# Attention weights transposed by DMA instead of TensorE, and a new order of the pieces with little elementwise work on GpSimd

## The chip, the core and the metric

The kernel runs on one core of a Trainium2 chip. TensorE (PE in the profile; PEld is its loading of weights) multiplies matrices into PSUM, VectorE (DVE), ScalarE (ACT) and GpSimd (POOL) work elementwise, SyncE (SP) and GpSimd issue most DMAs. Each engine takes its own instructions in order, and engines wait for each other through semaphores. The metric is the device time of one execution in microseconds (us); lower is better.

## What is computed

For each of 8 batches and 8 heads, x (512 x 64) reads the state (32 x 64) through a softmax, and the state reads x through another. Both results together are the 4352 tokens of a feed-forward layer with a squared relu. Cut to what matters:

```python
scores = scale * (x @ state.T)            # rows: softmax over the 32 states
xread  = softmax(scores) @ state
scores2 = scale * (state @ x.T)           # columns: softmax over the 512 positions
sread  = softmax(scores2) @ x
tokens = concat(xread, sread)             # per batch 512 + 32 rows of 512
out = (s * relu(tokens @ w_in)**2 + b) @ w_out
```

The second softmax, over the columns of the scores, is the one that the change touches.

## The kernel before, in words

The kernel is cut into pieces, each a small function in a table (`pieces`, near the end), and a list of words, `ORDER`, nine strings long, says in which order they are emitted. Each engine gets its instructions in that order; a letter at a word's end (A, V, G) says on which engine an elementwise piece runs. The framework sets the semaphores.

Per batch b, and with 128 partitions throughout:

- x is loaded twice on GpSimd's DMA queue: as `xh` (for the scores; piece x, L188) and as `xn` (positions on partitions; piece xn, L197, four DMAs of 128 KB). Two buffers each.
- Row softmax: `xT` (DVE transposes 32 x 32 blocks, L302), `T` (scores, PE), `U`, `mu`, `D`, `E1`, `z`, `At`, `A` on DVE and ACT (Dm and At sometimes on GpSimd, L336 and L357).
- Column softmax: `nm`, `nms`, `E2` (exponentials with row sums, ACT, L390), `a2` (the weights, normed, 128 x 1024 fp16, DVE, L397 and L399). Then the weights must have positions on partitions: `aps` turns 128 x 128 blocks on PE against an identity (eight matmuls into a PSUM bank, L141 by the helper), `a2T` copies the bank to SBUF (L156, on ACT seven times, on DVE once), and `V` multiplies with xn (PE tile vps). `srd` copies the result (ACT, L435).
- The state is multiplied with w_in once (`M`, PE tile mps, and `Mc`, its copy to SBUF, L156), so layer 1 is two matmuls of 512 columns for each 128 features: piece `l.b.f` (L472) with its relu on ACT (L476). `s.b.f.n.E` squares n such blocks (L482 on DVE and GpSimd, L480 on ACT).
- Layer 2: batches 0 and 1 plainly (`L`, L516, four pieces for each row block; `out` evicts and stores). Batches 2 to 7 by a scheme with seven products of half blocks instead of eight: `S.b.i.h.E` makes sums of blocks (L586), `P.b.u` is one product in halves (14 pieces of eight matmuls, PE tiles opf_X, opf_Y, opf_W), `ev` evicts a bank after a product (DVE, L615), `put` stores (SP). The bank X is used by four products one after the other, each continuing what is in it: a product waits for the eviction before it.
- At the end the 256 state rows go through the same two layers (`lsr`, `ssr`, `S_sr`, `P_sr`, `ev_sr`).

DMAs on SP (all stores of results but the last few) and on GpSimd (all loads but the first) each stand in the list's order on their queue.

Of the kernel before, what the change touches and what calls it, by code (L numbers as in the profile page):

```python
# [11 lines left out]
FP16 = mybir.dt.float16  # L12
# [70 lines left out]
def kernel(  # L83
# [321 lines left out]
    def at_aps(b):  # L405
        at[b]["aps"] = aps = blocks(two_banks(f"aps_{b}", FP16), 0)
        for g in range(NG):
            for c in range(SCH):
                transp(aps[:, SCH * g + c], at[b]["a2"][:, g, P * c : P * c + P])

    def at_a2T(b, e):
        copy(e, sm(b, "a2T", [P, NG * SCH, P], FP16, apool, 2), at[b]["aps"])
# [97 lines left out]
    ops_t = {}  # L510

    def layer2(tag, rr, q):
        if q == 0:
            ops_t[tag, rr] = ps_o.tile([P, DM], FP32, name=f"ops_{tag}_{rr}", tag="po")
        for f in range(4 * q, 4 * q + 4):
            nc.tensor.matmul(  # L516
                ops_t[tag, rr],
                G_t[tag][:, f, P * rr : P * rr + P],
                w_out_f(f),
                start=(f == 0),  # L520
                stop=(f == NKF - 1),
            )
# [74 lines left out]
    def product(b, u):  # L597
# [3 lines left out]
        first, last = bank not in [p[0] for p in PRODUCTS[:n]], bank not in [p[0] for p in PRODUCTS[n + 1 :]]  # L601
        lhs = block(b, *lhs) if lhs else fast(b, "S3")
        for k in range(4 * h, 4 * h + 4):
            w = fast_w[rhs][:, k] if isinstance(rhs, str) else w_block(*rhs)(k)
            for rr in range(2):
                mm(
                    fast(b, bank)[:, rr], lhs[:, k, P * rr : P * rr + P], w,
                    start=(first and k == 0 and rr == 0), stop=(last and k == NKF // 2 - 1 and rr == 1), skip=True,
                )
# [50 lines left out]
    def bias_sum(q):  # L660
        if q == 0:
            cps_t.append(two_banks("cps")[:, 0, :])
# [106 lines left out]
```

## Time and profile before

| | |
|---|---|
| time, median of 3 runs | 217.82 us (217.42 to 217.86) |
| span of the profiled execution, first to last instruction | 215.7 us |
| time outside the span | about 2.1 us, from the median of the runs; the profiled execution has no other time of its own |
| PE busy | 205.8 us |
| DVE busy | 179.6 us |
| ACT busy | 158.0 us |
| POOL busy (DMA issues among it) | 86.9 us |
| DMA packets | 22.43 MB in 23658 packets |

The profile gives for each engine the time in which one of its instructions ran. Rows of groups read: line of the kernel, engine, operation, output and input tile, shapes, count; then busy us and mean ns of one; then the idle time just before them and who ended it. Rows of the chain of work that ended last read: start, length, what. A row of the waits reads: who waited for whom, us in total, times, longest. Matmuls overlap in the records, so a mean of one matmul is longer than the time by which the next one follows; the chain shows the latter.

### The profile page before, as it was taken

To read this page: it belongs to the slowest core of one execution; us is meant where nothing else is said; L and a number is where in the kernel's file an instruction comes from. 1 tells how busy PE (TensorE), PEld (TensorE's weight loads), DVE (VectorE), ACT (ScalarE), POOL (GpSimd) and SP (SyncE) were. 2 spreads that over 40 slices of the span, in tenths; PEclk is the share of its full clock that TensorE was granted. 3 is DMA by queue.
4 is the path that set the end of the run, shared out by engine and by line. 5 is a ranking of instruction groups with operands and counts; after the bars stand their busy time and mean duration, and the time that the engine had idled before them with its cause. 6 is when DMAs were issued, how large, how long until landed. Compare 5 with 4: busy or idle time off the path is not lost.

```text
span 215.7 us, 4829 instructions
## 1 busy us (share of the span) xinstructions
PE 205.8 (95%) x1955; PEld 130.0 (60%) x1955; DVE 179.6 (83%) x277; ACT 158.0 (73%) x260; POOL 86.9 (40%) x94
## 2 busy tenths in 40 slices
PE   7489999999999999999999999999999999999992
PEld 2134343344444448767677677677766777888881
DVE  2997899999998799969998999999986874593661
ACT  4598886899899788799999887779768475734300
POOL 8554126445093033157437057007223308916400
PEclk9969999999999999999999999999999999999999
DMA  6999998127849719523900939608902600440045
GB/s 153 175 207 206 196 206 146 41 63 106 137 106 140 133 20 171 68 50 64 162 24 2 187 112 115 82 17 145 221 8 46 144 11 0 102 97 0 5 147 145
DMA packets 23658, 22.43 MB, mean 104 GB/s; under 512 B 4436, under 2 KB 17492, under 8 KB 23636
## 3 DMA queue, kind: packets, MB, share of 16 engines
q0 software_dynamic: 16848, 12.52, 41.3%
q1 hardware_dynamic: 5504, 8.66, 14.9%
q10 hardware_dynamic: 1284, 0.95, 1.7%
q8 instruction: 15, 0.25, 0.5%
q14 instruction: 7, 0.06, 0.1%
HBM read 25.72 MB, written 8.91 MB: 161 GB/s over the span
## 4 chain that ended last, share of the span: by engine, by line
PE 91%; DMA 3%; ACT 2%; POOL 1%; DVE 1%; issue 0%; POOLq 0%
PE hps L472 25%; PE opf_X L141 20%; PE ops L516 13%; PE opf_W L141 10%; PE opf_Y L141 5%; PE mps L141 5%; DMA w_in<-in_moe_w_in_dram 3%; PE hps_sr L472 3%; PE vps L141 2%; PE aps L141 2%; PE ops_sr_X L141 2%; PE T_None L141 2%; ACT M L156 1%; PE hph L141 1%; PE ops_sr_W L141 1%; PE dps L683 1%
## 5 line engine op out<-in xcount | busy, mean ns | idle before, releaser
L476 ACT ACTIVATE r<-hps 128x512 f16<-128x512 f32 x120 | 68.8, 603 | 25.6 <-PE hps L472 22.3
L472 PE MATMUL hps<-A,M 128*128 128x512 f16 x240 | 65.6, 380 | 0.1
L141 PEld LDWEIGHTS <-g 128*128 128x128 f16 x576 | 56.0, 98 | 15.2 <-issue 0.9
L472 PEld LDWEIGHTS <-M 128*128 128x128 f16 x240 | 21.4, 98 | 19.8 <-issue 6.0
L482 POOL TENSOR_TENSOR g<-r 128x1024 f16<-128x1024 f16 (+1 forms) x9 | 21.3, 2372 | 27.0 <-ACT r L476 22.8
L156 ACT CAST M<-mps 128x1024 f16<-128x1024 f32 x29 | 29.2, 1013 | 2.3 <-PE mps L141 1.9
L516 PE MATMUL ops<-w_out,g 128*128 128x512 f16 x128 | 30.7, 379 | 0.0
L197 POOL DMA_DIRECT2D xn<-in_x_dram x32 | 18.7, 604 | 14.8 <-PE vps L141 14.0
L141 PE MATMUL opf_X<-w_T,g 128*128 128x256 f16 x192 | 24.1, 273 | 0.0
L482 DVE TENSOR_TENSOR g<-r 128x1024 f16<-128x1024 f16 (+1 forms) x30 | 22.1, 754 | 1.6 <-ACT r L476 1.6
L586 DVE TENSOR_TENSOR g<-g 128x1024 f16<-128x1024 f16 (+1 forms) x31 | 22.1, 728 | 0.2
L516 PEld LDWEIGHTS <-g 128*128 128x128 f16 x128 | 12.4, 98 | 14.9 <-POOL g L482 0.2
L615 DVE SCALAR_TENSOR_TENSOR osx<-opf_X,sb_bc,bias_bc 128x512 f32<-128x512 f32 x18 | 13.3, 740 | 7.7 <-PE opf_X L141 7.4
L357 POOL TENSOR_TENSOR At<-E,rz 128x1024 f16<-128x1024 f16 x4 | 7.7, 1914 | 21.6 <-DVE rz L348 21.6
L480 ACT ACTIVATE g<-r 128x1024 f16<-128x1024 f16 (+1 forms) x11 | 15.8, 1444 | 0.2
L141 PE MATMUL mps<-w_in,stT 64*32 64x512 f16 x256 | 13.0, 397 | 1.6 <-DMA w_in<-in_moe_w_in_dram 1.3
L586 POOL TENSOR_TENSOR g<-g 128x1024 f16<-128x1024 f16 (+1 forms) x3 | 8.3, 2768 | 15.4 <-PE opf_X L141 8.1
L141 PE MATMUL opf_W<-w_out,g 128*128 128x256 f16 x96 | 12.4, 273 | 0.0
L141 PE MATMUL opf_W<-w_T,g 128*128 128x256 f16 x96 | 12.3, 273 | 0.0
L141 PE MATMUL opf_X<-w_out,g 128*128 128x256 f16 x96 | 12.1, 273 | 0.0
L141 PE MATMUL opf_X<-w_T,S 128*128 128x256 f16 x96 | 11.8, 273 | 0.0
L141 PE MATMUL opf_Y<-w_out,g 128*128 128x256 f16 x96 | 11.8, 273 | 0.0
(102 smaller groups left out, 310.4 us busy)
## 6 DMA issues: line engine op xcount, KB each, us to landing
out_dram<-osx SPq DMA_DIRECT2D x44, 128.0 KB, 2.4
xn<-in_x_dram POOLq DMA_DIRECT2D x32, 128.0 KB, 6.7
xh<-in_x_dram POOLq DMA_DIRECT2D x14, 256.0 KB, 5.2
w_in<-in_moe_w_in_dram POOLq DMA_DIRECT2D x8, 256.0 KB, 9.2
w_out<-in_moe_w_out_dram POOLq DMA_DIRECT2D x4, 512.0 KB, 13.3
out_dram<-osb SPq DMA_DIRECT2D x16, 64.0 KB, 1.9
out_dram<-osb SPq DMA_DIRECT2D x8, 128.0 KB, 2.4
xf<-in_x_dram SPq DMA_DIRECT2D x2, 256.0 KB, 3.7
```

The costliest lines, as they stand in the source:

```text
L141: return nc.tensor.matmul(out, lhsT, rhs, start=start, stop=stop, tile_position=tp, is_transpose=is_transpose, skip_group_check=skip,)
L156: (engine.copy if engine is nc.scalar else engine.tensor_copy)(out, in_)
L197: nc.gpsimd.dma_start(out=xn_t[b][32 * jh : 32 * jh + 32].rearrange("t h c d -> t h (c d)"), in_=x[b].rearrange("h (t jh c) d -> jh t h (c ...
L357: e.tensor_tensor(out, E1, over_n(rz), ALU.mult)
L472: nc.tensor.matmul(hps, lhsT, rhs, start=(i == 0), stop=(i == len(terms) - 1))
L476: nc.scalar.activation(R_t[tag, q][:, i], hps, AF.Relu)
L480: nc.scalar.activation(g, r, AF.Square)
L482: e.tensor_mul(g, r, r)
L516: nc.tensor.matmul(ops_t[tag, rr], G_t[tag][:, f, P * rr : P * rr + P], w_out_f(f), start=(f == 0), stop=(f == NKF - 1),)
L586: e.tensor_tensor(out, x, y, op)
L615: nc.vector.scalar_tensor_tensor(out, fast(b, name[0]), s_bc, out if plus else bias, ALU.mult, ALU.add)
L683: nc.tensor.matmul(dps, ones16[:, :P], ones16, start=True, stop=True)
```

## The change

Three things change.

1. `aps` and `a2T` are replaced by one piece, `tr`: one DMA on SP's queue that transposes the 128 x 1024 weights from SBUF to SBUF into the same tile a2T. It waits for a2 (DVE) and for the buffer of a2T (two of them; the V two batches of that order before). `V` waits for its landing.
2. `ORDER` is a new list. Its first words, up to the first pieces of layer 1 of batch 0, stay; all later pieces stand in another order, and most letters G are now V or A. GpSimd keeps one Dm and one At besides its DMAs. The transposes stand in the list away from the words of the xn loads.
3. So that the quarters of a layer-2 sum and the halves of a product can come in any order, the pieces count visits: the first visit of a bank starts the accumulation, the last one ends it.

Cut to its core:

```diff
-    def at_aps(b):
-        at[b]["aps"] = aps = blocks(two_banks(f"aps_{b}", FP16), 0)
-        for g in range(NG):
-            for c in range(SCH):
-                transp(aps[:, SCH * g + c], at[b]["a2"][:, g, P * c : P * c + P])
-
-    def at_a2T(b, e):
-        copy(e, sm(b, "a2T", [P, NG * SCH, P], FP16, apool, 2), at[b]["aps"])
+    def at_tr(b):
+        a2T = sm(b, "a2T", [P, NG * SCH, P], FP16, apool, 2)
+        nc.sync.dma_start_transpose(out=a2T, in_=at[b]["a2"].rearrange("p g s -> p (g s)"))
...
+    def visit(*key):
+        visits[key] = visits.get(key, 0) + 1
+        return visits[key]
...
     def layer2(tag, rr, q):
-        if q == 0:
+        v = visit("L", tag, rr)
+        if v == 1:
...
-                start=(f == 0),
-                stop=(f == NKF - 1),
+                start=(v == 1 and f == 4 * q),
+                stop=(v == NKF // 4 and f == 4 * q + 3),
```

The places of the list that the prediction walks through, in the changed order (the fifth string, around V.5.2, and the seventh, around V.6.0):

```
... l.4.7 nms.6.V s.4.6.2.A mu.6 P.3.6 E2.6.1 a2.2 P.3.7 E2.6.0 ev.3.X2 S.3.4.1.V tr.2 l.4.14 z.5 s.4.12.4.A
ev.3.W1 S.3.4.0.V xn.6 P.3.8 P.3.9 s.4.4.2.A l.4.8 l.4.11 M.5.1.1 ev.3.X3 At.5.V V.5.2 ...

... a2.0 tr.6 l.5.6 P.4.13 s.5.6.2.A l.6.2 s.5.12.2.A xn.0 Mc.6.1.A l.6.1 P.4.12 P.4.10 l.6.3
Mc.6.3.V P.4.11 tr.0 l.6.0 S.5.3.0.V P.5.0 S.5.1.0.V E1.7 ev.4.X4 s.5.14.2.V l.6.12 l.6.10 V.6.0 ...
```

The numbers of instructions that change engine, before and after: squares of 1024 columns on ACT 6 and 30, on DVE 27 and 10, on GpSimd 7 and 0; squares of 2048 on ACT 5 and 6, on DVE 3 and 4, on GpSimd 2 and 0; copies of M on ACT 29 and 25, on DVE 3 and 7; At on DVE 3 and 6, on GpSimd 4 and 1; sums of blocks on GpSimd 7 and 0; transposing matmuls 64 and 0.

More of the change, by code (lines that the diff above doesn't have):

```diff
@@ L508, in layer1_sr @@
         layer1("sr", f, [(w_in_f(k, f), srdT[:, k].rearrange("p n b -> p (n b)")) for k in range(NK)], B * Ns)
-    ops_t = {}
+    ops_t, visits = {}, {}
+    def visit(*key):
+        visits[key] = visits.get(key, 0) + 1
+        return visits[key]
     def layer2(tag, rr, q):
-        if q == 0:
+        v = visit("L", tag, rr)
+        if v == 1:
             ops_t[tag, rr] = ps_o.tile([P, DM], FP32, name=f"ops_{tag}_{rr}", tag="po")
@@ L600, in product @@
         bank, lhs, rhs = PRODUCTS[n]
-        first, last = bank not in [p[0] for p in PRODUCTS[:n]], bank not in [p[0] for p in PRODUCTS[n + 1 :]]
+        v, visits_all = visit("P", b, bank), 2 * sum(p[0] == bank for p in PRODUCTS)
         lhs = block(b, *lhs) if lhs else fast(b, "S3")
@@ L607, in product @@
                     fast(b, bank)[:, rr], lhs[:, k, P * rr : P * rr + P], w,
-                    start=(first and k == 0 and rr == 0), stop=(last and k == NKF // 2 - 1 and rr == 1), skip=True,
+                    start=(v == 1 and k == 4 * h and rr == 0),
+                    stop=(v == visits_all and k == 4 * h + 3 and rr == 1), skip=True,
                 )
@@ L660, in bias_sum @@
     def bias_sum(q):
-        if q == 0:
+        v = visit("cps")
+        if v == 1:
             cps_t.append(two_banks("cps")[:, 0, :])
@@ L667, in bias_sum @@
                 cps[32 * c : 32 * c + 32, :], ones16[:, 0:32], w_out_f(f),
-                start=(f < 4), stop=(f >= NKF - 4), tp=(0, 32 * c),
+                start=(v == 1), stop=(v == NKF // 4), tp=(0, 32 * c),
             )
@@ L728 @@
         "E1": at_E1, "z": at_z, "At": at_At, "A": at_A, "nm": at_nm, "nms": at_nms, "E2": at_E2, "a2": at_a2,
-        "aps": at_aps, "a2T": at_a2T, "V": at_V, "srd": at_srd, "M": at_M, "Mc": at_Mc,
+        "tr": at_tr, "V": at_V, "srd": at_srd, "M": at_M, "Mc": at_Mc,
         "lh": layer1_half, "sh": square_half, "l": layer1_x, "s": square, "lsr": layer1_sr,
```

117 rows, old and new, of the table ORDER are left out of this document.

## The prediction, made before the changed kernel was run

> **What bounds the kernel now.** I read four views, from the whole to the place. First the page: busy times, and the chain of work that ended last.
>
> ```profile
> span 215.7 us, 4829 instructions
> PE 205.8 (95%) x1955; PEld 130.0 (60%) x1955; DVE 179.6 (83%) x277; ACT 158.0 (73%) x260; POOL 86.9 (40%) x94
> PE 91%; DMA 3%; ACT 2%; POOL 1%; DVE 1%; issue 0%; POOLq 0%
> ```
>
> TensorE (PE) carries nine tenths of the chain. A busy PE is not yet a PE that never waits, so the second view is PE's waits after the head (from 25 us on), and the third the busy times by stage.
>
> ```profile
> PE mps L141 <- DVE M L156: 0.4, 1, 0.4
> ```
>
> ```profile
> core 0: us, PE busy (x) PEld busy (x) DVE busy (x) ACT busy (x) POOL busy (x), PEclk, DMA share, GB/s
> 25.00:160.00 135.00, 134.90 (x1284) 80.81 (x1284) 126.88 (x184) 115.55 (x184) 53.79 (x61) 1.00 0.62 104
> 160.00:211.60 51.60, 51.60 (x505) 41.44 (x503) 33.34 (x57) 24.90 (x49) 20.43 (x10) 1.00 0.25 62
> 211.60:216.00 4.40, 0.02 (x1) 0.00 (x0) 0.48 (x1) 0.00 (x0) 0.00 (x0) 1.00 0.44 121
> ```
>
> After the head PE waits for anybody once, for 0.4 us, and its clock is granted in full (1.00). From 25 to 211.6 us the time is the sum of PE's pieces, and nothing else. VectorE (DVE) is close behind: in 25 to 160 us it is idle for 135 - 126.88 = 8.1 us, ScalarE (ACT) for 19.5. So a change here is worth the PE work that it removes, less the waits that it brings back to PE. The last 4.4 us are one DVE instruction and a store; the change leaves that end as it is (the last product, its eviction, its store).
>
> **The change, part by part.** *The transposes leave PE.* Eight pieces named aps go, one for each batch, and nothing else leaves PE or comes to it: all other matmuls are the same ones in another order. In the chain in order of time each such piece stands with its own cost (the first, the dearest and the last of the eight):
>
> ```profile
> 55.57 0.45 PE aps L141 x8
> ...
> 104.49 0.55 PE aps L141 x8
> ...
> 178.14 0.45 PE aps L141 x8
> ```
>
> 8 x 0.45 = 3.6 us (3.7 with the dear one). All eight stand on the chain, one behind the other with PE's other work, so this comes off in full as long as PE stays fed. It is the only term that the change gains.
>
> *The copies out of PSUM, and GpSimd's elementwise work.* I counted instructions of each form on each engine in the changed kernel against the one before, and priced them with these rows:
>
> ```profile
> L156 ACT COPY a2T<-aps 128x1024 f16<-128x1024 f16 x7 | 7.1, 1015 | 0.0
> L156 ACT CAST M<-mps 128x1024 f16<-128x1024 f32 x29 | 29.2, 1013 | 2.3 <-PE mps L141 1.9 <-PE hps L472 0.3
> L480 ACT ACTIVATE g<-r 128x1024 f16<-128x1024 f16 x6 | 6.2, 1054 | 0.1
> L480 ACT ACTIVATE g<-r 128x2048 f16<-128x2048 f16 x5 | 9.6, 1912 | 0.1
> L480 ACT ACTIVATE g_sr<-r_sr 128x512 f16<-128x512 f16 x4 | 2.4, 625 | 0.6 <-PE opf_X L141 0.6
> L156 DVE CAST M<-mps 128x1024 f16<-128x1024 f32 x3 | 3.7, 1219 | 0.5 <-PE mps L141 0.5
> L357 DVE TENSOR_TENSOR At<-E,rz 128x1024 f16<-128x1024 f16 x3 | 3.9, 1303 | 0.1
> L482 DVE TENSOR_TENSOR g<-r 128x1024 f16<-128x1024 f16 x27 | 18.6, 703 | 1.6 <-ACT r L476 1.6
> L482 POOL TENSOR_TENSOR g<-r 128x1024 f16<-128x1024 f16 x7 | 13.9, 1990 | 17.0 <-ACT r L476 12.8 <-issue 4.2
> L482 POOL TENSOR_TENSOR g<-r 128x2048 f16<-128x2048 f16 x2 | 7.4, 3708 | 10.0 <-ACT r L476 10.0
> ```
>
> ACT: 24 more squares of 1024 (25.3 us), one more of 2048 (1.9), six more small ones (3.8), four casts of M fewer (-4.1), seven copies of a2T fewer (-7.1), one small copy fewer (-0.6): **+19 us**, to about 177. DVE: four more casts of M (4.9), three more At (3.9), seven more sums of blocks (about 4.9 at the 0.70 of a square of the same shape, the double one counted twice and the small ones half), one more square of 2048 (1.2), but 17 squares of 1024 fewer (-12.0) and three small ones (-1.3); with two small copies about **+1 us**, to about 181. GpSimd loses 22 squares, sums and At and keeps one At and one Dm. It was no bound: these two rows alone waited 22.8 us for ACT.
>
> This work lies beside PE, and its cover is PE's own stream. It costs nothing while each engine finishes its share before PE needs it. Total load leaves room (177 and 181 of 216), so what counts is the densest stretch. That is the list's fourth and fifth strings (first S.2.3.0 to last Mc.5.1). Records of one engine overlap at their ends; how fast instructions really follow each other is seen in the timeline of each engine, two relus and two sums of 1024 in a row:
>
> ```profile
> 66.79 1.08 ACT L476 ACTIVATE r<-hps 128x512 f16<-128x512 f32 x2
> ```
>
> ```profile
> 103.76 1.28 DVE L586 TENSOR_TENSOR g<-g 128x1024 f16<-128x1024 f16 x2
> ```
>
> Two relus of 0.60 take 1.08, so one follows another after 0.5: I take 0.1 off each ACT row; 0.08 off each DVE row in the same way. PE's pieces, from the chain again (two layer-1 pieces, one product, two M pieces):
>
> ```profile
> 54.71 0.86 PE hps L472 x4
> ...
> 88.68 0.87 PE opf_X L141 x8
> ...
> 93.91 0.56 PE mps L141 x16
> ```
>
> In that stretch PE has 25 products (21.9), 31 layer-1 pieces (13.3), three layer-2 pieces at two layer-1 pieces' cost (2.6) and about 6 us of M, T and V: 43 to 44 us. ACT has 31 relus (15.5), six casts (5.5), six squares of 1024 (5.7), six of 2048 (10.9) and some 6 us of exponentials and small copies: also 43 to 44. DVE's list there, added in the same way, gives the same. All three are full for 44 us. Before the change DVE ran at 126.88 / 135 = 94% without making PE wait; now ACT has that level too and the two pass work to each other. PE's waits there I bound from below at 0 (what the densest stage before showed, but for 0.4) and from above at about 5 (the 19 us that ACT gets, less the 19.5 that it had idle, would fit exactly; a quarter of it in the wrong place would not). I take **1 us**, near the row that shows a full engine costing almost nothing.
>
> *The transposing DMA.* Instead of eight matmuls and a copy, SP issues one DMA of 256 KB from SBUF to SBUF, and the piece V waits for its landing. The trace of before has no transposing DMA. The nearest rows, DMA issues with size and median time to landing:
>
> ```profile
> out_dram<-osx SPq DMA_DIRECT2D x44, 128.0 KB, 2.4
> xn<-in_x_dram POOLq DMA_DIRECT2D x32, 128.0 KB, 6.7
> xf<-in_x_dram SPq DMA_DIRECT2D x2, 256.0 KB, 3.7
> stn<-in_state_dram POOLq DMA_DIRECT2D x1, 192.0 KB, 12.7
> ```
>
> From 2.4 (it can gain nothing below zero: its landing is only ever waited for) to 12.7; I take 3.7, the row of the same queue and size. Does that fit? The tightest place is V.5.2, behind tr.2. After a2.2 DVE's queue has ev.3.X2 (0.74 by the row below), for which the product P.3.8 waits; then PE has P.3.8 and P.3.9 (1.75), two layer-1 pieces (0.86) and M.5.1.1 (0.3) before V.5.2.
>
> ```profile
> L615 DVE SCALAR_TENSOR_TENSOR osx<-opf_X,sb_bc,osx 128x512 f32<-128x512 f32 x6 | 4.5, 742 | 2.0 <-PE opf_X L141 1.8
> ```
>
> So V.5.2 comes at the earliest 0.74 + 1.75 + 0.86 + 0.3 = 3.7 us after a2.2, and a landing of 3.7 costs nothing. Behind tr.0, tr.7 and tr.1 PE has 6.9 to 7.4 us of pieces between the place of a2 and that of V; less a2's own 0.9 that is 6 us. Behind tr.3, tr.4, tr.5 and tr.6 there is more. Queued behind a transpose on SP stand only stores of results; the next batch's first eviction waits for those, some 5 us of PE's pieces later where it is closest, and a store lands in 2.4. On GpSimd the loads of xn now stand almost alone and can start earlier. All this I cost at 0.
>
> Sum against the profiled execution: span 215.7 - 3.6 + 1.0 = 213.1. The median of the runs shown, 217.82, lies 2.1 above that span, so 217.8 - 2.6 = **215.2 us**. With no wait at all and a few M and T pieces standing closer together it would be 213.8.
>
> **The rivals.** *The landing comes late (slower).* A landing of d us after a2 makes PE wait d - 3.7 at V.5.2 and d - 6 at each of V.6.0, V.7 and V.1. Nothing remains of the 2.6 us from d = 6.2 on (2.5 + 3 x 0.2 = 3.1; at 6.1 it is 2.7). At 6.7, the row of the xn loads that may run beside it, the waits are 3.0 + 2.1 = 5.1: 215.2 + 5.1 = 220.3. For it: no row shows a transpose, and both rows of GpSimd's queue lie above 6. Against it: both rows of SP's queue, on which the transposes are issued, lie under 4. I give it 0.25.
>
> *Far later.* At 12.7, the slowest row, the waits are 9.0 + 20.1 = 29: 244 us, and each further us adds four. [...] 0.05.
>
> *ACT and DVE become the bound.* PE's waits in the dense stretch reach the 3.6 us of the gain: 217.8, or somewhat above at the bound of 5 (219.2). For it: all three engines full for 44 us. Against it: DVE was as full before and cost PE 0.4. 0.12.
>
> *The transposes were hidden anyway* is excluded: all eight stand in the chain with their full 0.45.
>
> **How the numbers follow.** Forecast (213.8 to 217.0): 0.58. Late landing 0.25, far later 0.05, ACT and DVE the bound 0.12. A measurement of this kernel can tell about 0.2% (0.4 us). Faster: the forecast and a little of the third rival, 0.60. Same: half of that rival, 0.06. Slower: the rest, 0.34. The range runs from 213.8 to 222.0: below it nothing is reachable with the matmuls that remain, above it lie the far case and the part of the first rival with d over 7.1, together under 0.2. The forecast's own range is 213.8 to 217.0.
>
> **What would show it.** Right: the chain without aps and with no DMA named a2T in it; PE's waits after 25 us sum to about 1 us, on ACT's r and DVE's osx or g; a2T lands within 4 us of its issue; ACT near 177 less its overlaps, GpSimd under 45. Wrong: waits of the vps matmuls for a2T (the first rival, by its landing time), long waits of hps for r or of opf for g or S (the third), or transposes that slow the loads or stores beside them, for which I have no row.

## The result, and the profile after

The changed kernel took 214.99 us (median of 4 runs, 214.72 to 215.54) against 217.84 (217.42 to 218.11) of the kernel before in the same measurement: a ratio of 0.987, 95% interval 0.985 to 0.989, so faster by 1.3%. Its profiled execution has a span of 212.9 us. Here and in the table of the experiments a ratio leaves out runs more than 1.5% above the fastest of the same kernel; medians and ranges do not.

First the page of the changed kernel, in the order of the prediction: span and instructions, busy times, and the chain of work that ended last by engine.

```profile
span 212.9 us, 4690 instructions
PE 202.8 (95%) x1891; PEld 126.6 (59%) x1891; DVE 179.5 (84%) x272; ACT 170.9 (80%) x279; POOL 42.8 (20%) x72
PE 77%; DVE 9%; ACT 7%; DMA 3%; issue 1%; SPq 1%; DVEq 0%
```

PE has 64 instructions fewer (the transposing matmuls) and 3.0 us less busy time. ACT has 12.9 more, GpSimd 44.1 less. PE's share of the chain fell from 91% to 77%, which looks like a new bound and is none: the chain passes through ACT, DVE and one store wherever PE is released just in time. How long PE really waits stands in its waits from 25 us on:

```profile
PE mps L140 <- ACT M L155: 0.2, 1, 0.2
PE opf_X L140 <- DVE osx L615: 0.2, 1, 0.2
```

0.33 us in all (0.17 and 0.16), as little as the one wait before the change (0.37). The busy times by stage (columns as before: PE, PEld, DVE, ACT, POOL, granted clock, DMA share, GB/s):

```profile
25.00:160.00 135.00, 134.65 (x1250) 78.99 (x1248) 127.79 (x179) 124.93 (x199) 30.14 (x49) 1.00 0.68 115
160.00:209.00 49.00, 48.45 (x475) 39.43 (x473) 32.36 (x55) 27.89 (x53) 0.00 (x0) 1.00 0.31 77
```

From 25 to 160 us ACT's idle time went from 19.5 to 10.1 us, DVE's from 8.1 to 7.2. Both could be filled that far while PE stayed fed.

The new operation, by its tile: the durations on the queue (ns, least, median, most), then the landings.

```profile
L406 SPq DMA_TRANSPOSE a2T<-a x8: 1232/1278/2179, 58.7 to 166.8; - x8
DMA to landing us min/median/max: 2.7/2.8/7.5
```

No matmul waited for it. Of the seven landings that the trace has, six took 2.7 to 3.7 us. The one of 7.5 us is that of batch 4, issued at 80.06 beside two loads of xh (issued at 78.1 and 78.7, landed at 82.0 and 84.5) and right behind two stores of 128 KB on its own queue, the second of which landed at 86.7; its V is far away in the list.

Where the 2.8 us of span went: the last matmul group starts at 207.58 instead of 210.75, 3.17 us earlier. The rows of the eight pieces add up to 3.7 (7 x 0.45 + 0.55). The waits after the head are the same, so they are no part of the 0.5 us between the two. PE's first 112 matmuls are the same in both kernels, and the last of these starts at 18.03 before and at 18.29 after: 0.26 us were lost there, in a stretch where both kernels do the same. The other 0.3 us lie in small differences of PE's later pieces; no single cause of them is shown. Behind PE another 0.4 us was given back, where the last stores landed later. Rows of before, then of after, with size and median landing:

```profile
out_dram<-osr ACTq DMA_DIRECT2D x2, 128.0 KB, 2.3
out_dram<-osr SPq DMA_DIRECT2D x2, 128.0 KB, 2.5
```

```profile
out_dram<-osr SPq DMA_DIRECT2D x2, 128.0 KB, 2.9
out_dram<-osr ACTq DMA_DIRECT2D x2, 128.0 KB, 3.1
```

### The profile page after: what moved, and what is told of

It reads as the page before. It is cut to its first block, busy times and chain, and to the rows that moved or that the text cites. A ratio compares the mean times of both kernels' runs of the same rounds, so it can differ in the third digit from the quotient of the medians.

```text
span 212.9 us, 4690 instructions
## 1 busy us (share of the span) xinstructions
PE 202.8 (95%) x1891; PEld 126.6 (59%) x1891; DVE 179.5 (84%) x272; ACT 170.9 (80%) x279; POOL 42.8 (20%) x72
## 2 busy tenths in 40 slices
DMA packets 32107, 24.54 MB, mean 115 GB/s; under 512 B 12884, under 2 KB 25940, under 8 KB 32084
## 4 chain that ended last, share of the span: by engine, by line
PE 77%; DVE 9%; ACT 7%; DMA 3%; issue 1%; SPq 1%; DVEq 0%
PE hps L466 21%; PE opf_X L140 17%; PE ops L515 13%; PE opf_W L140 7%; PE opf_Y L140 4%; PE hps_sr L466 3%; ACT g L474 3%; PE mps L140 3%; DMA out_dram<-osx 3%; PE dps L684 2%; PE ops_sr_X L140 2%; PE T_None L140 2%; DVE Dm L335 1%; DVE g L476 1%; ACT r L470 1%; PE vps L140 1%
## 5 line engine op out<-in xcount | busy, mean ns | idle before, releaser
L474 ACT ACTIVATE g<-r 128x1024 f16<-128x1024 f16 (+1 forms) x36 | 42.8, 1210 | 0.2
L466 PEld LDWEIGHTS <-M 128*128 128x128 f16 x240 | 22.2, 98 | 18.9 <-issue 5.4
L515 PE MATMUL ops<-w_out,g 128*128 128x512 f16 x128 | 31.9, 379 | 0.0
L585 DVE TENSOR_TENSOR g<-g 128x1024 f16<-128x1024 f16 (+1 forms) x34 | 24.3, 715 | 3.2 <-PE opf_Y L140 1.8
L155 ACT CAST M<-mps 128x1024 f16<-128x1024 f32 x25 | 25.7, 1035 | 0.9 <-PE mps L140 0.9
L476 DVE TENSOR_TENSOR g<-r 128x1024 f16<-128x1024 f16 (+1 forms) x14 | 11.6, 830 | 3.1 <-ACT r L470 2.9
L140 PE MATMUL mps<-w_in,stT 64*32 64x512 f16 x256 | 12.5, 407 | 1.2 <-DMA w_in<-in_moe_w_in_dram 1.0
L470 ACT ACTIVATE r_sr<-hps_sr 128x256 f16<-128x256 f32 x16 | 6.1, 383 | 9.0 <-PE hps_sr L466 8.7
L140 PE MATMUL opf_Y<-w_out,g 128*128 128x256 f16 x96 | 12.5, 273 | 0.0
L184 POOL COPY ahead<-xT 1x2 f16<-1x2 f16 x5 | 2.5, 507 | 42.6 <-DVE xT L301 42.6
L140 PEld LDWEIGHTS <-S 128*128 128x128 f16 x96 | 9.3, 98 | 2.6 <-issue 0.4
```

The costliest lines, as they stand in the source:

```text
L140: return nc.tensor.matmul(out, lhsT, rhs, start=start, stop=stop, tile_position=tp, is_transpose=is_transpose, skip_group_check=skip,)
L155: (engine.copy if engine is nc.scalar else engine.tensor_copy)(out, in_)
L184: nc.gpsimd.tensor_copy(ahead, at[b - 1]["xT"][0:1, 0, 0])
L466: nc.tensor.matmul(hps, lhsT, rhs, start=(i == 0), stop=(i == len(terms) - 1))
L470: nc.scalar.activation(R_t[tag, q][:, i], hps, AF.Relu)
L474: nc.scalar.activation(g, r, AF.Square)
```

## The experiments

The theory: PE is the bound, the eight pieces stood on its chain, and the gain is their 3.6 us, whatever the order. Rivals: the new order (or GpSimd's lighter load) is what gains, or it is needed so that nothing is lost again. The kernel before took 217.8 to 218.0 us beside every one of these runs. Ratios are to it, with 95% intervals. The waits are PE's from 25 us on, in the profiled execution.

| kernel | list | transposes | time us (range) | ratio | PE's waits us |
|---|---|---|---|---|---|
| before | old | PE | 217.84 | | 0.4 |
| after | new | DMA, SP | 214.99 | 0.987 [0.985, 0.989] | 0.4 |
| e1 | old, stores earlier | DMA, SP | 222.96 (222.5 to 223.1) | 1.023 [1.021, 1.025] | 6.1 |
| e5 | old, four stores earlier | DMA, SP | 228.37 (227.3 to 229.4) | 1.048 [1.045, 1.051] | 10.1 |
| e9 | old | DMA, ACT | 222.01 (218.6 to 226.8) | 1.012 [1.007, 1.016] | 3.1 |
| e10 | old, transposes earlier | DMA, ACT | 220.92 (220.6 to 224.5) | 1.014 [1.012, 1.015] | 4.5 |
| e12 | old, two buffers of a2 | DMA, ACT | 221.96 (217.8 to 227.3) | 1.017 [1.014, 1.020] | 2.8 |
| e2 | new | PE | 223.59 (223.2 to 223.8) | 1.026 [1.024, 1.028] | 4.8 |
| e7 | old, GpSimd's pieces moved | PE | 227.68 (227.6 to 228.1) | 1.045 [1.043, 1.047] | 8.2 |
| e3 | new | DMA, SP, twice | 218.11 (216.8 to 219.2) | 1.001 [0.999, 1.003] | 3.8 |
| e4 | new, a load beside each | DMA, SP | 219.11 (218.0 to 220.2) | 1.006 [1.003, 1.008] | 2.8 |
| e8 | new | DMA, ACT | 217.80 (217.4 to 220.9) | 1.001 [0.998, 1.003] | 2.9 |
| e6 | new, four At on GpSimd | DMA, SP | 231.23 (230.9 to 231.4) | 1.061 [1.059, 1.063] | 12.5 |
| e11 | new, three squares on GpSimd | DMA, SP | 216.30 (215.9 to 216.6) | 0.993 [0.991, 0.994] | 1.6 |

The ratio of e12 is the one on record; its two shortest runs, 217.81 and 220.76 us, are 1.000 and 1.013, so nothing below rests on it.

### e1: the transposes by DMA in the old order

The piece tr of the change, put into the list of before at the places of aps; the words a2T are gone, GpSimd keeps all its pieces. A store behind a transpose on SP would here be waited for by the very instructions that the transpose waits for, so every put stands right behind the last eviction of its half.

```diff
-    def at_aps(b): ...
-    def at_a2T(b, e): ...
+    def at_tr(b):
+        a2T = sm(b, "a2T", [P, NG * SCH, P], FP16, apool, 2)
+        nc.sync.dma_start_transpose(out=a2T, in_=at[b]["a2"].rearrange("p g s -> p (g s)"))
```

> The order of before, GpSimd's elementwise work and all, with only the transposes changed: each aps becomes a transposing DMA, each a2T copy goes; the stores of a finished half block stand right behind its last eviction, so that no transpose on SP stands ahead of a store that its own batch's DVE work waits for. Theory (the gain is PE's 3.6 us and nothing else): 217.84 - 3.6 = 214.2 us, between 213.8 and 215.2, PE waits after 25 us under 1 us. Rival (the new order is what makes the transposes pay, in the old one they land late or beside loads): V waits for a2T, 216 us or more.

It took 222.96 us: the theory that the gain comes in any order falls. PE's waits, then the wait of DVE that stands behind the first of them:

```profile
PE opf_X L133 <- DVE osx L602: 5.1, 1, 5.1
...
DVE osx L602 <- DMA out_dram<-osx: 5.9, 1, 5.9
```

The landings of the transposes are not it (median 2.8). One eviction waited for the store of the same buffer from the batch before: those stores were issued at 145.6 to 147.5, behind four others, and landed 5 to 6.4 us later, beside eight loads of xn. My early stores may have a share in that, so e5 leaves most of them where they were. There is a second loss: the clock granted to PE after the wait (seventh figure of a row, after the five engines' busy times).

```profile
150.00:153.00 3.00, 0.00 (x0) 0.00 (x0) 0.00 (x0) 0.32 (x1) 0.10 (x1) 1.00 1.32 252
153.00:156.00 3.00, 1.23 (x6) 0.84 (x6) 2.00 (x6) 0.00 (x0) 0.00 (x0) 0.77 1.02 141
156.00:159.00 3.00, 3.00 (x16) 1.91 (x15) 2.55 (x5) 1.34 (x2) 0.00 (x0) 0.66 0.40 90
```

0.23 x 3 + 0.34 x 3 = 1.7 us more. The last matmul group starts 4.4 us later than before the change: -3.6 + 5.7 more of waits + 1.7 = 3.8, and some 0.6 in small pieces.

### e5: the same, with only four stores moved

Only the stores go ahead of a transpose that would otherwise close a circle of waits (put.2.0.1 ahead of tr.2, put.3.1.0 and put.3.1.1 ahead of tr.0, put.5.0.1 ahead of tr.1).

> Once more the order of before with transposing DMAs, since the earlier try had moved all stores forward and its one long wait (5.3 us at 149 us) was for stores that stood behind four others and beside eight loads of xn. Now only the four stores move that must stand ahead of a transpose. Theory (the gain is PE's 3.6 us, the order adds nothing): 214.2 us, between 213.8 and 215.2. Rival (in an order not made for it SP's single queue and the loads beside it eat the gain): V or opf wait 1.5 us or more in all, 216 to 219.

228.37 us, above the theory and above the rival's range. PE's largest waits, the longest one 4.9 us, are for evictions:

```profile
PE opf_W L133 <- DVE osx L602: 5.8, 3, 4.9
PE opf_X L133 <- DVE osx L602: 2.0, 1, 2.0
```

The chain in order of time names what was ahead of the longest:

```profile
180.99 0.45 PE hps L459 x2
181.43 0.03 SPq L399
181.46 0.04 issue
181.50 0.60 SPq L611
...
183.42 2.37 DMA out_dram<-osx
...
185.91 0.76 DVE osx L602
186.68 0.04 issue
186.72 1.72 PE opf_W L133 x8
```

L399 is the transpose of batch 1, which stood at SP's head for 9.5 us until its a2 was done at 180.2; four stores (L611) stood behind it, and the eviction waits for one of those. The store itself lands in 2.4 us; it started late. So on SP this transpose held back what stood behind it until its input was there. In the old order stores that are soon needed stand there; the prediction looked at this for the new order only, and costed it at nothing.

### e9, e10, e12: the old order, the transposes on ACT's queue

No store on SP stands behind a transpose now. e9 has tr at the places of a2T, e10 at the places of aps. e12 is e9 with two buffers for a2, paid for with a row buffer.

```diff
-        nc.sync.dma_start_transpose(...)
+        nc.scalar.dma_start_transpose(...)
# e12 besides:
-        ... sm(b, "a2", [P, NG, S], FP16)
+        ... sm(b, "a2", [P, NG, S], FP16, None, 2)
-    opool = ... bufs=4
+    opool = ... bufs=3
```

> The order of before, all of GpSimd's work kept, and each transposing DMA issued from ACT's queue at the place of the a2T copy that it replaces: no store on SP stands behind a transpose, and ACT gives 1.25 us of issuing for a copy of 0.9. Theory (the gain is PE's 3.6 us where no queue holds anything up): 214.2 to 215.5. Rival (the old order loses by transposes on any queue, by late landings beside its loads): 216 or more, with V waiting for a2T.

> The same, with each transpose at the place of the old aps, some PE pieces earlier: a2T is there earlier, but ACT waits for a2 with relus behind it. Theory: within 1 us of the other, 214.2 to 216.5, V's waits smaller and the relus' larger.

e9 took 222.01 us, e10 220.92: both miss. In e9 a new wait shows, on DVE:

```profile
DVE a L391 <- DMA a2T<-a: 4.3, 2, 2.9
```

There is one buffer for a2. While PE read it, it was free after 0.45 us; the DMA kept it until it had landed, here 4.2 us from the issue, and DVE's next a2, and all that stood behind it, waited, 2.9 us at the longest. e12 takes that away.

> The old order with the transposes on ScalarE's queue once more, and two buffers for the weights a2 instead of one, so that VectorE's next a2 need not wait until the DMA has read the last one (4.3 us in two waits, the longest 2.9, in the run with one buffer). The space comes from the row buffers osb, three instead of four, which may cost the first batches' evictions a wait of their own (with four they waited 1.0 once). If the held buffer is what the old order loses the 3.6 us to: no wait of a2 for a2T, the wait of opf_W for VectorE's osx (1.8) gone, 214.2 to 216.5 us. If it is the transfers beside each other, or VectorE's load as such: still 217.5 to 222 us, with PE's waits for osx as before.

The wait for a2T is gone from DVE, PE's waits for osx fell from 2.1 to 1.3 us, and the two shortest runs from 218.56 and 221.19 to 217.81 and 220.76 (V now waited 0.5 us for a2T). The median over all runs did not move (221.96): the held buffer is real, and it is not what keeps the old order from 214, which no run came near. In both kernels the profiled execution was the shortest of its six, so the traces bear on that one alone; what makes others up to 9.5 us longer no trace shows, and it stays open. In e10 the wait of PE was for a store again:

```profile
PE opf_X L133 <- DVE osx L602: 2.5, 2, 2.1
...
DVE osx L602 <- DMA out_dram<-osx: 2.9, 1, 2.9
```

### e2, e7: the order and GpSimd's work alone

e2 is the changed kernel with the transposes back on PE: aps and a2T.A instead of tr, each at the next place where a PSUM bank is free for it. e7 is the kernel before with 23 of GpSimd's 24 elementwise pieces moved to ACT or DVE, each at its place in the list.

> The new order with PE's eight transposes and ACT's copies put back, each at the next place after the transposing DMA's where the PSUM bank is free. Theory: 214.99 + 3.6 for PE = 218.6 us, and up to 1.5 more since ACT gets 8 copies of about 0.9 us back in the stretch where it is full: 218.4 to 220. Rival (the new order gains by itself, DVE and GpSimd no longer in each other's way): 217.8 or under.

> The kernel before, transposes on PE, with all but one of GpSimd's 24 elementwise pieces moved in place: squares to ACT (about 11 us), the rest to DVE (about 12 us). Theory (ACT and DVE have no room for it in an order made for GpSimd): PE waits 2 to 6 us after 25 us, 219 to 224. Rival (GpSimd was never needed): 217.4 to 218.2.

e2 took 223.59 us, 8.6 more than after and above the theory's 218.4 to 220. 3.6 of that are the matmuls, 4.4 are waits that PE has besides:

```profile
PE aps L134 <- ACT M L149: 2.4, 3, 1.5
PE opf_X L134 <- DVE osx L614: 1.3, 2, 0.8
PE mps L134 <- ACT a2T L149: 0.6, 1, 0.6
```

The bank that aps needs is shared with M, and ACT, nearly full in this order, frees it late. So this order with the transposes on PE at these places does not gain but lose: 2.6 us of the waits are aps for that bank and 0.6 M for the a2T copy, and the DMA needs neither the bank nor the copy. An order made for these transposes on PE was not tried. e7, 227.68 us, is above its theory's 219 to 224. It loses through eight different waits of at most 2.0 us each in total, 4.0 us of them for ACT's squares: in the old order, emptying GpSimd is no gain by itself either.

### e3, e4: how much landing the new order bears

e3 issues every transpose twice, so that a2T is ready about 5.6 us after a2. e4 adds a load of 176 KB on GpSimd's queue that is released by the same a2.

```diff
+        for _ in range(2):                                   # e3
             nc.sync.dma_start_transpose(...)
# e4:
+        side = xpool.tile([P, 11, D], FP16, ..., bufs=1)
+        nc.gpsimd.tensor_copy(side[0:1, 0, 0:2], at[b]["a2"][0:1, 0, 0:2])
+        nc.gpsimd.dma_start(out=side..., in_=x[b, 0:4]...)
```

> Each transpose is issued twice, the second waiting for the landing of the first, so a2T is there 5.6 us after a2 instead of 2.8. Theory with the slack as the changed kernel's trace shows it (V.5.2 4.7 us after its a2, V.6.0 5.8, V.7 5.5, V.1 7.4): waits of about 1 us in all, 215.9 us. By the prediction's slack of 3.7 and three times 6: 1.9 us, 216.9. Rival (landings are hidden at any length that occurs): 215.0.

> Beside each transpose one more load on GpSimd's queue, 128 partitions of 704 values into a tile that nothing reads, released by the same a2. In the changed kernel seven transposes land in 2.7 to 3.7 us and the one beside two loads of xh in 7.5. Theory (a load beside it is what makes a transpose slow): all eight land in 5 to 8 us, V waits for some 1 to 8 us in all, 216 to 223 us. Rival (the one slow landing had another cause): landings stay at 2.8 and the time at 215.0 to 215.3.

e3 took 218.11 us, 3.1 more than after, where at most 1.9 were expected. PE's waits, and one of DVE:

```profile
PE opf_X L140 <- DVE osx L616: 2.4, 2, 1.4
PE vps L140 <- DMA a2T<-a: 1.4, 2, 1.2
...
DVE a L398 <- DMA a2T<-a: 3.0, 2, 2.7
```

The wait of vps for a2T is the prediction's first rival in kind: batch 2's a2T was read 6.5 us after its a2, after a wait of 1.2 us, and batch 7's landed 5.6 after, a wait of 0.2. Of the waits for osx 1.4 us came at 91.7, behind DVE's wait for the held a2 buffer (2.7 us, until 90.4); the other 1.0 came at 154.4, where an eviction waited 2.0 us for a store. In e4 the landings went up:

```profile
DMA to landing us min/median/max: 3.1/5.0/7.8
```

from 2.7/2.8/7.5, and the time to 219.11 us. With a load beside it a transpose landed later, if not always by as much as expected (5 to 8 us for all). The expected waits of V did not come: batch 2's a2T landed at 117.52 and was read at 117.56. So the 4.1 us over after are not shown to be the landing's: PE's waits are for M and osx, none for a2T, and GpSimd's own loads stand behind the added work, which waits for a2.

### e8, e6, e11: queue and GpSimd in the new order

e8 issues the transposes of the changed kernel from ACT's queue, e6 puts At of batches 2, 3, 5 and 7 back on GpSimd, e11 puts three squares of batch 7, behind GpSimd's last load, there.

```diff
-  nc.sync.dma_start_transpose(...)     # e8
+  nc.scalar.dma_start_transpose(...)
-  At.2.V ... At.3.V ... At.5.V ... At.7.V     # e6
+  At.2.G ... At.3.G ... At.5.G ... At.7.G
-  s.7.4.2.A ... s.7.6.2.A ... s.7.10.2.A      # e11
+  s.7.4.2.G ... s.7.6.2.G ... s.7.10.2.G
```

> The changed kernel with the eight transposes issued from ACT's queue instead of SP's. One issue holds SP for 1.25 us, so ACT loses 8 x 1.25 = 10 us plus its waits for a2, in the stretch where it is full. Theory: PE waits for relus, 220 to 228. Rival (issues from ACT are cheap, and off SP no store stands behind a transpose): 214.5 to 215.5.

> The changed kernel with four At (batches 2, 3, 5, 7) back on GpSimd, where before had them; nothing else moves. DVE gets 4 x 1.2 us back, each At takes 1.9 instead of 1.3. Theory (PE stays fed either way; emptying GpSimd is no gain of its own): 214.7 to 215.4. Rival (GpSimd's elementwise work slows DVE or comes late and that costs): 216 or more.

> The changed kernel with three squares of batch 7 (1024 columns each) on GpSimd instead of ACT, behind its last load, so that no load stands behind them. Theory (what made four At on GpSimd cost 16 us was the loads of xn queued behind them, and the row softmax that waited, not GpSimd working beside DVE): 214.7 to 215.6. Rival (GpSimd's elementwise work slows DVE or is too slow at any place): 216 or more.

e8, 217.80 us, lies between the theory's range and the rival's. All recorded landings are 2.7 to 2.8, and each issue holds ACT's queue:

```profile
L406 ACTq DMA_TRANSPOSE a2T<-a x8: 1247/1248/1341, 56.6 to 171.6; - x8
```

8 x 1.25 = 10 us, as much as ACT had idle from 25 to 160 us. But PE waited only 0.3 us for a relu. The 2.8 us over after go with 2.5 us more of PE's waits, and most of these are for evictions:

```profile
PE opf_X L140 <- DVE osx L615: 2.0, 2, 1.8
...
DVE osx L615 <- DMA out_dram<-osx: 2.9, 1, 2.9
```

The eviction at 153.1 waited for a store, as in e1, e3, e5 and e10 at 152 to 154. ACT also reaches some transposes late: the fifth was issued at 136.9 instead of 125.1, and DVE then waited 1.4 us for the a2 buffer. That ACT's lost 10 us as such are the cause, as the theory had it, is not shown. SP, which issues the stores and does no elementwise work, is the better queue in this order (214.99 us against 217.80).

e6, 231.23 us, was expected at 215 and is 16 us off. PE's longest wait, and GpSimd's:

```profile
PE vps L133 <- DMA xn<-in_x_dram: 6.4, 1, 6.4
...
POOL At L349 <- DVE rz L340: 36.0, 3, 15.7
```

At waits up to 15.7 us for DVE at the head of GpSimd's queue, and the loads of xn behind it wait with it. PE stood from 69 to 75 us, and then its clock was low for 7 us (seventh figure):

```profile
75.00:78.00 3.00, 2.58 (x36) 1.55 (x37) 0.07 (x1) 0.00 (x0) 1.23 (x3) 0.50 1.21 208
78.00:82.00 4.00, 4.00 (x16) 1.68 (x15) 0.75 (x1) 2.58 (x5) 1.11 (x2) 0.79 1.24 203
```

That is 2.3 us more. A second wait, of 3.0 us at 130, was for At itself, which came late on GpSimd (DVE's A waited 3.2 us for it). The 20 matmuls behind it took 4.46 us on the chain (130.5 to 135.0), where such pieces take 0.97 + 0.87 + 0.87 = 2.7 elsewhere in it: another 1.7. With 12.1 us more of PE's waits this makes up the 16. e11 puts elementwise work on GpSimd where no load stands behind it and takes 216.30 us. That is far from e6, so most of e6's loss goes with what stands behind the work in GpSimd's queue. But e11 misses its theory and is 1.3 us over after, and its trace shows the rival, GpSimd's work slowing DVE. Here are DVE's a2 of batch 1 in the changed kernel, then the same in e11, GpSimd's squares beside it, and PE's longest wait:

```profile
165.12 0.62 DVE L398 TENSOR_SCALAR a<-E,q 128x512 f16<-128x512 f16 x2
```

```profile
165.57 3.20 DVE L391 TENSOR_SCALAR a<-E,q 128x512 f16<-128x512 f16 x2
164.82 3.79 POOL L469 TENSOR_TENSOR g<-r 128x1024 f16<-128x1024 f16 x2 [14.37 <-PE opf_X L133]
PE opf_Y L133 <- DVE osx L608: 1.0, 1, 1.0
```

The two instructions took 3.20 us instead of 0.62 beside the squares, the eviction behind them came late, and PE waited 1.0 us for it, most of what its waits grew by. So a GpSimd without elementwise work has some value of its own where PE soon needs what DVE does; in e11 it is this one place.

None of these kernels beats the changed one.

## Why the prediction was right, point by point

The forecast of 215.2 us stands against 214.99, and the mechanism is the one that was forecast. That the two agree to 0.2 us is luck in part. The sum for the span, 215.7 - 3.6 + 1.0 = 213.1, added 1.0 us of waits that did not come, and took as unchanged what cost 0.9: 0.5 in PE's other pieces (0.26 of it in the head) and 0.4 behind PE. Measured is 215.7 - 3.7 + 0.5 + 0.4 = 212.9.

- **The transposes leave PE, 3.6 us in full.** Right: all eight pieces stood on the chain, their rows are gone, and nothing waits in their place. The last matmul group starts 3.17 us earlier, for the reasons given with the result.
- **PE's waits, taken as 1 us more.** They did not grow (0.33 after 0.37), and they were for M and osx: ACT was filled to 93% from 25 to 160 us and DVE to 95% at no cost. Waits of the size of the bound of 5 us came with other kernels: e2 and e7 have 4.8 and 8.2 us.
- **The landing, taken as 3.7 us.** Measured 2.8 as the median, so the row of the same size on the same queue was the right neighbour and slightly dear. The sign "lands within 4 us" failed once, with 7.5 us for batch 4, where nothing was near enough to wait. In the same profile xf, a plain load of the same size on the same queue, took 3.6 (median of two). The far case, 12.7 us, did not come: the issue held the queue for 1.28 us (median) and the longest landing was that of 7.5.
- **The slack at V.** The prediction counted 3.7 us from a2 to V.5.2 and 6 at each of the three others. V.5.2 and V.6.0 each do two batches, and the one that waits for the late transpose comes second, half a us into the piece. From a2's end to the matmul that waits there were 5.3 us for batch 2, 6.3 for batch 0, 5.5 for batch 7 and 7.4 for batch 1. With the landings that this run shows, about 2.5 us or more were left everywhere. e3 shows that the rival was real in kind (1.4 us of waits for a2T), and e4 that a load beside is enough to bring it near. By these numbers a landing of 7.5 us like that of batch 4 would have cost about 7.5 - 5.3 = 2.2 us, most of the gain, for batch 2: an estimate, no run shows it.
- **Stores on SP, costed at 0 because a store lands in 2.4.** Nearly right and close: at 150 us an eviction waited 1.2 us for a store that landed late beside loads, and PE 0.16. The same place cost PE 1.0 to 5.1 us in e1, e3, e5, e8 and e10.
- **The tail, taken as unchanged.** It became 0.4 us longer by stores that landed 0.4 to 0.8 us later.
- **Loads: ACT 177 less overlaps, DVE 181, GpSimd under 45.** Measured 170.9, 179.5, 42.8.
- **What the prediction left out.** Two costs of the DMA that the new order avoids, and that show in five other kernels: SP's head held by a transpose that waits for its input (9.5 us in e5), and the a2 buffer held until the landing (DVE's a2 waited 3.0 us in e3, 1.7 in e8, 4.3 in e9, 2.2 in e10). My theory after the result, that the order was no part of the gain, fell with e1, e5, e9, e10 and e12. Shown is: in the changed kernel PE's eight pieces are gone and no wait came in their place; the order with PE's transposes (e2), GpSimd's relief alone (e7) and the DMA alone (e1, e5, e9, e10, e12) do not gain. Why the old order with ACT's queue and two buffers still varies between 217.8 and 227.3 us is not settled.

## What to carry to other kernels

Work that leaves the engine on the chain is worth its rows in that chain, but only in an order in which nobody waits for the new path: look at what stands behind a waiting DMA on its queue, at who needs its source buffer next, and at which loads run beside it. Here two engines were filled to 93 and 95% beside a saturated PE at no cost, in an order made for it; GpSimd's work moved to the same engines in the order made for something else cost 9.8 us (e7). Elementwise work that waits should not stand ahead of loads on the queue that issues them (in e6 At waited up to 15.7 us there, and PE 6.4 for xn), and elementwise work on GpSimd can slow VectorE beside it (in e11 two instructions took 3.20 us instead of 0.62).

## What the runs showed of the hardware that was not expected

- A transposing DMA of 256 KB from SBUF to SBUF landed in 2.7 to 2.8 us in five of seven records on SP's queue (after; the others 3.7 and 7.5) and in all on ACT's (e8), and in 3.1 to 7.8 us (median 5.0) with a load beside each (e4). It held the issuing queue for 1.28 us on SP and 1.25 on ACT (medians). It moved in small packets: under 512 B there were 4436 before and 12884 after, 8448 more, 1056 for each transpose.
- Some waits of PE cost more than their length. In e10 one of 2.15 us (151.3 to 153.4) was followed by 3 us at a granted clock of 0.52 (155 to 158):

```profile
153.00:155.00 2.00, 1.56 (x12) 1.29 (x12) 1.96 (x6) 0.00 (x0) 0.00 (x0) 0.86 1.29 273
155.00:158.00 3.00, 3.00 (x13) 1.50 (x11) 3.00 (x4) 1.65 (x3) 0.00 (x0) 0.52 1.38 213
```

0.14 x 2 + 0.48 x 3 = 1.7 us on top of 2.15. The longest waits were followed by a lower clock too: 0.77 and 0.66 after 5.1 us in e1, 0.61 after 4.9 in e5, 0.50 and 0.79 after 6.4 in e6. After waits of 1.8 us in e8 and in e9 it stayed at 1.00; behind one of 2.0 in e5 the 16 matmuls of opf_X took 1.91 us on the chain, where 1.75 to 1.85 is usual in that run.
- Stores of 128 KB that land in 2.4 us in the median (after) took 5.0 to 6.7 when issued at 144 to 148 us, beside the eight loads of xn, in e1 and in the changed kernel; in the changed kernel this cost PE 0.2 us, in e1 5.1.
- Two instructions on VectorE that take 0.62 us together took 3.20 beside squares on GpSimd (e11). In the kernel before, two of its instructions beside GpSimd's sums and squares took 1.23 and 1.60 us where such ones take 0.7; PE did not wait for them there.
